# The first 12 units of an mLSTM cell with its MLP: hand-written order against a list schedule

## The chip, the cores and the metric

One core of a Trainium2 chip runs the whole program. The core has a tensor engine (TensorE, PE in the profile), a vector engine (VectorE, DVE), a scalar engine (ScalarE, ACT), a general engine (GpSimd, POOL) and a queue engine (SyncE, SP), each with its own queue of instructions that it works through in order. Transfers to and from memory (DMA) are handed out by SyncE, ScalarE or GpSimd. The metric is the device time of one execution in microseconds (us); less is better.

## The reference: an mLSTM cell, then an MLP with h - tanh(h)

Inputs are q, k, v and an output gate of shape (4, 8, 768, 40) (batches, heads, tokens, head size), gates i and f of shape (4, 8, 768), and the weights w_in (320 x 2048) and w_out (2048 x 320).

```python
for t in range(S):                       # per batch and head
    m_new = maximum(f[t] + m, i[t])
    f_stab, i_stab = exp(f[t] + m - m_new), exp(i[t] - m_new)
    C = f_stab * C + i_stab * outer(v[t], k[t])
    n = f_stab * n + i_stab * k[t]
    y[t] = sigmoid(o[t]) * (C @ q[t]) / maximum(abs(n @ q[t]), 1.0)
x = y as (3072 tokens, 320)
h = x @ w_in
out = (h - tanh(h)) @ w_out
```

All is float32 in the result. The weights arrive as 64-bit floating-point numbers, and the kernel turns their bits into float32 itself.

## The kernel before

**The cell in units.** The 768 tokens of a batch are cut into 6 chunks of 128; with 4 batches that makes 24 units (`NU`), unit n being chunk n // 4 of batch n % 4. Within a chunk the recurrence is written as matrix products. A unit goes through these steps:

- `load_unit` fetches its tiles: `kz`, `qz`, `v`, `k`, `o` and, from the second chunk on, `q2`.
- `scores`: 8 products of `kz` and `qz` into two banks (`ps`), then `mask` on VectorE writes the causal part to `P`.
- `prepare`: VectorE multiplies `v` with the gates' factors into `vs`, and lets the old state decay.
- `inter` (old state times q) and `intra` (`P` times `vs`): products into a bank `ph`.
- `open_gate` (sigmoid on ScalarE) and `gate` (VectorE: denominator, reciprocal, two products) give the unit's output `ys`.
- `update`: products of `vs` and `k` (`pc`), added to the state on VectorE.
- `turn`: three transposes of `ys` (`px`), copied by ScalarE to `xT`, the MLP's input for a group of two units.

The banks for `ph`, `pc`, `px` and the gates' products are the two of the pool `small` (`b0`, `b1`); every call takes the next one in turn.

**The gates.** `gate_rows` runs the scan for m on VectorE, and `gate_columns` turns the rows and makes the exponentials, both first for chunk 0 and then for chunks 1 to 5. VectorE, ScalarE and TensorE take turns in it.

**The weights.** The 2048 hidden features are cut into 16 blocks of 128, two of which are a pair p, 0 to 7. `convert` cuts each pair into five blocks (w_in in 256, 256 and 128 elements a partition, w_out twice in 320). Each block is fetched into `w64` and takes five VectorE steps (mask of the exponent, mask of the mantissa, `one`, `sign`, `product`) and two ScalarE steps (`w_r` and `w_e`). ScalarE's queue hands out the transfers of pair 0, GpSimd's those of the others.

**The MLP.** For a group g of two units (256 tokens) and a pair p, `up` makes h in the banks `ph_up`: four products over 128 features and two over 64. `shrink` makes h - tanh(h) as a polynomial: two squares on ScalarE (`z`, `q`) and two multiplies on VectorE (`gt`). `down` multiplies by w_out into `po`. For groups 0 to 3 the order of pairs is `RUNS`: it starts with group 0 and pair 0 and widens as units and weights become ready, so that a partial sum over some pairs is kept in `part` and added later. From group 4 to 10 all pairs of a group follow one another and `down_seven` replaces eight products by seven (`pS`); group 11 uses `down` again. Pairs are taken two at a time in 50 items; items 0, 1, 8 and 17 hold one. Items 0 to 17 are the 32 pairs of groups 0 to 3.

**What sets the order.** Each engine's order is the order in which the program writes its instructions; `Pinned` and `T` hold the framework to it. It is written in two ways. The start, units 0 to 2 with the gates and pair 0, is a list of calls by hand, with `awake(n)` in it: products of ones that nothing reads, of 512 columns, into the bank `ph0`. From then on a loop over items x writes `up` of item x and `down` of item x - 1 (`LAG` = 1), and `merge` lays other steps between them in proportion: those of the units (`cell_slot`, each spread over an interval of items), of the weights (spread over intervals before they are due) and of the gates. `Clock` delays single steps by a time counted in estimated matmul costs. From item 18 on, one bank of `small` is used for `pS`, and the units work with the other alone (`single`).

Of the kernel before, what the change touches and what calls it, by code (L numbers as in the profile page):

```python
# [59 lines left out]
L = 128  # L60
# [18 lines left out]
def kernel(  # L79
# [76 lines left out]

    B, NT, D, H, _ = qT.shape
# [85 lines left out]
    for n in range(2):  # L243
        load_unit(n, ("kz",))
        load_unit(n, ("qz",), A)
        load_unit(n, ("v",))
    load_gates(later)
    for name in "ko":
        for n in range(2):
            load_unit(n, (name,))  # L250


    ident = const.tile([128, 128], FP, name="ident")
# [31 lines left out]
    def awake(n):  # L285

        if not spare:
            spare.append(ps_h.tile([128, 512], FP, name="awake", tag="ph0"))
        row = diag.rearrange("p h t -> p (h t)")
        for _ in range(n):  # L290
            T.matmul(spare[0], row[:, 0:128], row[:, 0:512], start=True, stop=True)
# [13 lines left out]
    def gate_rows(c0, c1):  # L305

        t0, t1 = c0 * L, c1 * L
        at = slice(t0, t1)
        V.tensor_tensor_scan(out=m_sb[:, at], data0=f_sb[:, at], data1=i_sb[:, at],
                             initial=m_sb[:, t0 - 1:t0] if t0 else -1.0e30, op0=OP.add, op1=OP.max)  # L310
        if t0 == 0:

            V.memset(lf[:, 0:1], 0.0)
            t0 = 1
        V.tensor_tensor(out=lf[:, t0:t1], in0=f_sb[:, t0:t1], in1=m_sb[:, t0 - 1:t1 - 1], op=OP.add)
        V.tensor_tensor(out=lf[:, t0:t1], in0=lf[:, t0:t1], in1=m_sb[:, t0:t1], op=OP.subtract)
        V.tensor_tensor(out=i_sb[:, at], in0=i_sb[:, at], in1=m_sb[:, at], op=OP.subtract)


    def gate_columns(c0, c1, bank):  # L320
# [15 lines left out]

        def forget():
            V.tensor_copy(out=lfT[:, cs], in_=turned(0, lf))

        def admit():  # L340
            A.activation(out=ei[:, 2, cs], in_=turned(1, i_sb), func=AF.Exp)

        def since():
            V.tensor_single_scalar(inv[:, cs], sums_of(0, upto), 2 * DEEP, op=OP.max)
            V.tensor_reduce(out=least, in_=inv[:, cs].rearrange("p c n -> p (c n)"), axis=mybir.AxisListType.X, op=OP.min)
            A.activation(out=inv[:, cs], in_=inv[:, cs], func=AF.Exp, scale=-1.0)

        def until():
            A.activation(out=eS[:, cs], in_=sums_of(1, after), func=AF.Exp)
            V.tensor_tensor(out=ei[:, 0, cs], in0=ei[:, 2, cs], in1=inv[:, cs], op=OP.mult)  # L350
            V.tensor_tensor(out=ei[:, 1, cs], in0=ei[:, 2, cs], in1=eS[:, cs], op=OP.mult)

        def whole():
            half = sums_of(0, ones).rearrange("p c (b j two) -> p (c b) two j", two=2, j=HH)
            us = slice(c0 * B, c1 * B)
            A.activation(out=eT[:, us], in_=half[:, :, 1, :], func=AF.Exp)
            A.activation(out=eT[0:D, us], in_=half[0:D, :, 0, :], func=AF.Exp)
            V.tensor_single_scalar(least, least, TINY / DEEP, op=OP.mult)

        return forget, admit, since, until, whole  # L360


    w_in = const.tile([128, NK, DFF], FP, name="w_in")

    w_rest = const.tile([128, NP, 128], FP, name="w_rest")
    w_out = const.tile([128, NFF, DM], FP, name="w_out")

    def weights(dst, srcs, queue):
# [5 lines left out]
        def fetch():  # L374
            to = dst
            if src.dtype != FP:
                to = w["st"] = conv.tile([128, n], I64, name="w64", tag="w64", bufs=8)[0:p]
            for rows, cols, part in srcs:
                queue.dma_start(out=to[rows, cols], in_=part)

        def exponent():

            w["hi"] = w["st"].bitcast(I32).rearrange("p (n two) -> p n two", two=2)[:, :, 1]
            e = w["e"] = conv.tile([128, n], I32, name="w_e", tag="w_e", bufs=3)[0:p]
            V.tensor_single_scalar(e, w["hi"], 0x7FF00000, op=OP.bitwise_and)
            Clock.later(w["st"], 0.6, lambda: A.activation(out=e, in_=e, func=AF.Relu, scale=8.0, bias=rebias[0:p]))

        def mantissa():

            lo = w["st"].bitcast(U32).rearrange("p (n two) -> p n two", two=2)[:, :, 0]  # L390
            m, r = (conv.tile([128, n], I32, name=name, tag=name, bufs=3)[0:p] for name in ("w_m", "w_r"))
            w["m"], w["r"] = m.bitcast(FP), r.bitcast(FP)
            A.activation(out=w["r"], in_=lo, func=AF.Copy, scale=2.0 ** -52)
            V.tensor_scalar(out=m, in0=w["hi"], scalar1=0xFFFFF, scalar2=0x41000000, op0=OP.bitwise_and, op1=OP.bitwise_or)
# [5 lines left out]
        def sign():  # L400
            Clock.need(w["st"])
# [5 lines left out]
        if src.dtype == FP:  # L407
            return fetch, (), ()
        return fetch, (exponent, mantissa), (one, sign, product)

    WB = 2 * 128

    BLOCK = 5

    def convert():

        blocks = []
        for p in range(NP):
            queue = nc.gpsimd if p else A
            cols = slice(p * WB, (p + 1) * WB)  # L420
            fs = (2 * p, 2 * p + 1)
            every, slices = slice(0, 128), [slice(f * 128, (f + 1) * 128) for f in fs]
            blocks.append(weights(w_in[:, 0, cols], [(every, slice(0, WB), moe_w_in[0:128, cols])], queue))
            blocks.append(weights(w_in[:, 1, cols], [
                (every, slice(i * 128, (i + 1) * 128), moe_w_in[r:r + 128, slices[i]])
                for i, r in enumerate((FROM[2], FROM[1]))], queue))
            blocks.append(weights(w_rest[:, p, :], [
                (slice(i * HALF, (i + 1) * HALF), every, moe_w_in[r:r + HALF, slices[i]])
                for i, r in enumerate((FROM[1], FROM[2] + HALF))], queue))
            for f in fs:  # L430
                blocks.append(weights(w_out[:, f, :], [(every, slice(0, DM), moe_w_out[f * 128:(f + 1) * 128, :])], queue))
        steps = []
        for x in range(len(blocks) + 4):
            block = [blocks[i] if BLOCK <= i < len(blocks) else (lambda: None, (), ()) for i in (x, x - 2, x - 4)]
            steps.append([block[0][0], *block[2][2], *block[1][1]])
        return blocks[:BLOCK], steps

# [11 lines left out]
    def begin(n):  # L449
        t = un[n] = ld.pop(n)  # L450
        t["c"], t["b"] = divmod(n, B)
        t["hs"] = slice(t["b"] * H, (t["b"] + 1) * H)

        t["P"] = att.tile([L, 2, HH, L], FP, name="P", tag="P", bufs=4)
        t["qs"] = t.get("q2")
# [75 lines left out]
    def update(n, j):  # L531
        t = un[n]
        st = state[t["b"]][(t["c"] + 1) % 2]
# [3 lines left out]
        if j < HH - 1:  # L537
            return
# [7 lines left out]
    def turn(n, j):  # L546
# [4 lines left out]
        if j == NK:  # L551
            g, tt = divmod(n, GT)
            A.copy(out=xT[g % NX][:, :, tt * L:(tt + 1) * L], in_=t["px"])

    def cell_slot(s, o, x, single=False):


        steps = []
        if o is not None:
            prepare(o)  # L560
        if s is not None and s - 1 in un:
            prepare(s - 1)
# [4 lines left out]
        if x is not None and "turned" not in un[x]:  # L567
            turning = [(0.11, lambda j=j: turn(x, j)) for j in range(NK + 1)]
        else:
            turning = []  # L570
        if single:

            steps += turning
            if o is not None:
                for d in range(HH):
                    steps.append((0.22 if o >= B else 0.0, lambda d=d: inter(o, d)))
                    steps += [(0.22, lambda h=h: intra(o, h)) for h in (2 * d, 2 * d + 1)]
                steps.append((0.0, lambda: gate(o)))
                un[o]["turned"] = True
                pause = [(0.0, lambda: None)]  # L580
                steps += 5 * pause
                if o + B < NU:
                    steps += [(0.18, lambda j=j: update(o, j)) for j in range(HH)] + 4 * pause
                steps += [(0.11, lambda j=j: turn(o, j)) for j in range(NK + 1)] + 4 * pause
            return steps
        for d in range(HH):
            if o is not None:
                steps.append((0.22 if o >= B else 0.0, lambda d=d: inter(o, d)))
                steps += [(0.22, lambda h=h: intra(o, h)) for h in (2 * d, 2 * d + 1)]
                if d in (1, 2) and o + B < NU:  # L590
                    steps += [(0.18, lambda j=j: update(o, j)) for j in (2 * d - 2, 2 * d - 1)]
        if o is not None:
            steps.append((0.0, lambda: gate(o)))
        return steps + turning
# [10 lines left out]
    def sums_of_weights(p):  # L605
        t = wT[p] = conv.tile([128, 4, HM], FP, name="wT", tag="w64", bufs=8)
# [479 lines left out]
```

## Time and profile before

The median of three runs is 617.42 us (617.13 to 618.26). The profiled execution spans 614.3 us.

| engine | busy us | share | instructions |
|---|---|---|---|
| PE (matmul) | 564.4 | 92% | 3473 |
| PEld (weight load) | 472.7 | 77% | 3473 |
| DVE | 364.7 | 59% | 888 |
| ACT | 188.7 | 31% | 483 |
| POOL | 28.2 | 5% | 60 |

A float32 product shows as two matmul records, so "x24" for `ph_up` is 12 products. Most calls go through the helper at line 106 (VectorE and ScalarE) or line 129 (TensorE), so the profile is read by the names of tiles rather than by lines. In the profile's second part each digit is the busy share of one of 40 slices of 15.4 us, in tenths, and PEclk is the share of its full clock that TensorE was granted. In a table of stretches, "25.17 (x141)" is busy time and number of instructions. In a list of instructions the first number is the start, the second the time, and square brackets hold the idle time ahead of the instruction and what ended it.

### The profile page before, as it was taken

Reading aid. Unit: us, or ns where it says so; the run is one execution under the profiler, and the core shown is the slowest. Engines: PE = TensorE matmul, PEld = TensorE weight load, DVE = VectorE, ACT = ScalarE, POOL = GpSimd, SP = SyncE. Lnnn points to the kernel's source line nnn. Section 1 sums busy time; section 2 is a strip of 40 time slices with the busy share of each in tenths; the row PEclk is TensorE's granted clock in tenths of the full one; section 3 lists DMA queues with packets and bytes.
Section 4 is the critical chain, followed back from the end, with each engine's and each line's share of the span. In section 5 each row is a group of like instructions: output and inputs, shape, how many; then the busy total and the mean of one; then the engine's idle time right before and its main releaser. Section 6 shows DMA issues by size and latency. Waiting matters only on the chain.

```text
span 614.3 us, 9270 instructions
## 1 busy us (share of the span) xinstructions
PE 564.4 (92%) x3473; PEld 472.7 (77%) x3473; DVE 364.7 (59%) x888; ACT 188.7 (31%) x483; POOL 28.2 (5%) x60
## 2 busy tenths in 40 slices
PE   3948877899999899989999999999999999999996
PEld 1736766677777677767889899898988989888873
DVE  2686666666768855455876666556546456374421
ACT  1234333333435422321323232313132323133312
POOL 2021210001112000000000000000000000000000
PEclk7575589999999899999999999999999999999999
DMA  7653432323223301022211113011101000000000
GB/s 207 202 169 111 128 108 82 97 82 104 79 83 86 99 2 43 22 65 87 66 44 33 53 44 97 23 44 54 33 11 34 1 23 1 1 22 1 22 0 27
DMA packets 40868, 38.23 MB, mean 62 GB/s; under 512 B 3856, under 2 KB 38352, under 8 KB 40816
## 3 DMA queue, kind: packets, MB, share of 16 engines
q1 hardware_dynamic: 33000, 22.82, 12.8%
q0 software_dynamic: 2800, 9.18, 5.1%
q10 hardware_dynamic: 5016, 5.57, 2.7%
q8 instruction: 29, 0.48, 0.3%
q14 instruction: 23, 0.19, 0.1%
HBM read 33.62 MB, written 3.93 MB: 61 GB/s over the span
## 4 chain that ended last, share of the span: by engine, by line
PE 82%; DVE 12%; DMA 2%; issue 1%; ACT 1%; ACTq 0%; SPq 0%; DVEq 0%
PE ph_up L129 37%; PE pS L129 19%; PE po L129 11%; PE ph L129 8%; PE ps L129 4%; DVE gt L106 2%; PE pc L129 2%; DVE P L106 2%; PE px L133 2%; DMA kz<-in_kT 1%; PE awake L129 1%; DVE o L106 1%; DVE den L106 1%; DVE w_e L106 1%; DVE ys L106 1%
## 5 line engine op out<-in xcount | busy, mean ns | idle before, releaser
L129 PE MATMUL ph_up<-xT,w_in 128*128 128x256 f32 x768 | 206.8, 398 | 6.7 <-ACT xT L106 6.7
L129 PEld LDWEIGHTS ph_up<-xT,w_in 128*128 128x128 f32 x768 | 135.7, 194 | 20.4 <-ACT xT L106 7.2
L106 ACT ACTIVATE z<-ph_up 128x512 f32<-128x512 f32 (+1 forms) x100 | 57.1, 576 | 263.8 <-PE ph_up L129 180.0
L106 DVE SCALAR_TENSOR_TENSOR gt<-ph_up,z 128x512 f32<-128x512 f32 (+1 forms) x100 | 63.4, 663 | 99.4 <-ACT z L106 99.4
L129 PE MATMUL po<-w_out,gt 128*128 128x320 f32 x320 | 107.7, 459 | 1.4 <-DVE part L106 1.0
L129 PEld LDWEIGHTS ph<-vs,P 128*128 128x128 f32 x384 | 72.6, 212 | 20.0 <-issue 8.1
L106 DVE TENSOR_TENSOR P<-ps,upto 128x512 f32<-128x512 f32 x48 | 30.9, 686 | 75.8 <-PE ps L129 75.8
L129 PE MATMUL ph<-vs,P 128*128 128x41 f32 x384 | 65.5, 266 | 6.1 <-DVE vs L106 3.1
L129 PEld LDWEIGHTS po<-w_out,gt 128*128 128x128 f32 x320 | 55.4, 196 | 18.9 <-DVE part L106 3.5
L106 ACT ACTIVATE q<-z,tiny 128x512 f32<-128x512 f32 (+1 forms) x100 | 64.7, 701 | 0.0
L106 DVE SCALAR_TENSOR_TENSOR gt<-q,gt 128x512 f32<-128x512 f32 (+1 forms) x100 | 63.2, 661 | 0.0
L129 PE MATMUL pS<-wT,s 128*128 128x160 f32 x336 | 56.3, 304 | 0.0
L129 PE MATMUL ph_up<-xT,w_rest 64*128 64x256 f32 x384 | 55.5, 406 | 0.0
L129 PEld LDWEIGHTS pS<-wT,s 128*128 128x128 f32 x336 | 48.0, 190 | 0.0
L129 PEld LDWEIGHTS ph_up<-xT,w_rest 64*128 64x128 f32 x384 | 33.1, 187 | 14.2 <-issue 11.0
L106 ACT ACTIVATE w_e<-w_e,rebias 128x256 int32<-128x256 int32 (+2 forms) x40 | 20.3, 508 | 74.0 <-DVE w_e L106 73.9
L129 PE MATMUL pS<-w_out,gt 128*128 128x160 f32 x224 | 40.9, 314 | 0.0
L133 PE MATMUL px<-ident,ys 128*128 128x128 f32 x72 | 19.1, 291 | 19.5 <-DVE ys L106 18.7
L129 PEld LDWEIGHTS pS<-w_out,gt 128*128 128x128 f32 x224 | 32.0, 191 | 4.7 <-issue 4.3
L129 PEld LDWEIGHTS ph<-state,q 80*128 80x128 f32 x160 | 28.5, 195 | 6.5 <-issue 1.3
L129 PEld LDWEIGHTS ps<-qz,kz 40*128 40x128 f32 x384 | 28.9, 211 | 2.3 <-DVE P L106 0.8
L133 PEld LDWEIGHTS px<-ident,ys 128*128 128x128 f32 x72 | 10.2, 147 | 26.2 <-issue 22.2
(92 smaller groups left out, 562.9 us busy)
## 6 DMA issues: line engine op xcount, KB each, us to landing
w<-in_moe_w_out POOLq DMA_DIRECT2D x14, 320.0 KB, 3.3
kz<-in_kT SPq DMA_DIRECT2D x48, 80.0 KB
v<-in_v SPq DMA_DIRECT2D x24, 160.0 KB
k<-in_k SPq DMA_DIRECT2D x24, 160.0 KB
o<-in_o_gate SPq DMA_DIRECT2D x24, 160.0 KB
out<-ob ACTq DMA_DIRECT2D x24, 160.0 KB
qz<-in_qT SPq DMA_DIRECT2D x44, 80.0 KB
q<-in_qT SPq DMA_DIRECT2D x40, 80.0 KB
```

The source lines that it names most:

```text
L106: i = method(*args, **kwargs)
L129: return cls.keep(nc.tensor.matmul(*args, **kwargs))
L133: return cls.keep(nc.tensor.transpose(*args, **kwargs))
```

## The change

The part of the program up to item 17 gets its order from a list schedule. `Plan` holds operations, each with an engine (T, V, A, S for SyncE's loads, G for GpSimd's), an estimated duration, the operations it comes after, a rank, and buffers that it takes or gives back (`tokens`). `run` always takes the operation that can start first by the estimates, the lower rank among equals, and writes its instructions; so the written order of every engine follows from the plan. When TensorE has a gap in the plan, `idle` fills 60% of it with products of ones, which keep its clock up. The planned part covers units 0 to 11 (`PLANNED` = 12), the gates, all weights and items 0 to 17 but the last `down`; after it, the loop over items goes on from item 18 (`START`) with units 12 to 23, one unit to every two items.

Along with it:

- the weights of a pair are converted in two blocks of 640 elements a partition in place of five (`blocks_of`; w_in and the rest tile become one tile), all fetched through GpSimd's queue, with 4 buffers in place of 8;
- `v` of units 0 and 1 is fetched through GpSimd's queue, and `o` and `k` ahead of the later gates;
- `probe`, an exponential of one column at the start of ScalarE's queue, loads the activation table early;
- each step of `gate_rows`, `gate_columns`, `update`, `turn`, `shrink` and `down` can be called apart from the others, so that the plan can place it.

```diff
+    class Plan:
+        LAG = {"T": 0.25, "V": 0.07, "A": 0.12, "S": 1.7, "G": 1.9}
+        RATE = 0.23
...
+        def run(self, idle):
+            while self.todo:
+                t, _, _, op = min(((t, op["rank"], op["serial"], op) for op in self.todo if (t := self.start(op)) is not None),
+                                  key=lambda x: x[:3])
...
+                if op["engine"] == "T":
+                    idle(self.free["T"], t)
+                op["step"]()
+                op["end"] = self.free[op["engine"]] = t + op["us"]
...
-        load_unit(n, ("v",))
-    load_gates(later)
-    for name in "ko":
+        load_unit(n, ("v",), G)
+    for name in "ok":
         for n in range(2):
             load_unit(n, (name,))
+    load_gates(later)
...
+    probe = const.tile([128, 1], FP, name="probe")
+    V.memset(probe, 0.0)
+    A.activation(out=probe, in_=probe, func=AF.Exp)
...
-                to = w["st"] = conv.tile([128, n], I64, name="w64", tag="w64", bufs=8)[0:p]
+                to = w["st"] = conv.tile([128, n], I64, name="w64", tag="w64", bufs=4)[0:p]
...
+        return (weights(w_in[:, p, :], whole, nc.gpsimd),
+                weights(w_out[:, 2 * p:2 * p + 2, :].rearrange("p two n -> p (two n)"),
+                        [(every, slice(i * DM, (i + 1) * DM), moe_w_out[slices(2 * p + i, 1), :]) for i in range(2)], nc.gpsimd))
...
+    PLANNED = 12
+    START = item(FIRST * NP)
+    plan = Plan(small=("b0", "b1"), a=1, up=1, po0=1, po1=1, gt=2, z=1, P=4, vs=3, w64=4, w=2, ob=2)
...
+        u["scores"] = plan.add("T", 1.35, first_part, [u["qz"]], rank, [("a", held), ("P", held)])
+        u["mask"] = [plan.add("V", 0.68, lambda i=i: ready[1][i](), [u["scores"]], rank, give=[("a", held)] if i else ())
+                     for i in range(2)]
...
+        u["gate"] = plan.add("V", 1.5, lambda: gate(n), [op, u["open"], *of(n - 2, "turn")], rank, give=[("small", held)])
...
+            op = plan.add("G", 1.2 if k else 2.8, fetch, (), r, [("w64", held)], at=at, kb=655)
+            op = plan.add("V", 1.0, parts, [op], r, [("w", held)])
+            op = plan.add("A", 1.46, numbers, [op], r)
+            op = plan.add("V", 0.82, one, [op], r)
+            op = plan.add("V", 0.82, sign, [op], r, give=[("w64", held)])
+            converted[p, k] = plan.add("V", 0.82, product, [op], r, give=[("w", held)])
...
+    for x in range(START):
+        plan_item(x)
+    busy = []
+
+    def idle(t0, t1):
+        n = int((t1 - t0) * 0.6 / 0.215)
+        if n and not busy:
+            awake(n)
+        elif n and plan.tokens["a"] and plan.tokens["a"][0][0] <= t0:
+            stream(ps_a.tile([128, 512], FP, name="awake", tag="a0"), n)
+
+    plan.run(idle)
...
+    slots = [tuple(n if PLANNED <= n < NU else None for n in (s, s - 1)) for s in range(PLANNED, NU + 1)]
+    last = item((NG - 1) * NP) - 2.0
+    for i, slot in enumerate(slots):
+        x0, x1 = (START + (last - START) * j / len(slots) for j in (i, i + 1))
+        begins[int(x0)].append((slot, x0, x1))
```

The calls by hand at the start, `convert`, the spreading of weights over items and the two-bank form of `cell_slot` are removed.

## The prediction

> **What bounds the kernel now.** I read the span by slices first, then busy time by stage, then the order of TensorE's instructions inside a stage, and last the waits of the start. The slices show two regimes:
>
> ```profile
> PE   3948877899999899989999999999999999999996
> DVE  2686666666768855455876666556546456374421
> PEclk7575589999999899999999999999999999999999
> ```
>
> From slice 19 on TensorE (PE) is at 9 and its clock is full. In the first five slices (77 us) it is often idle and its clock is at 0.5 to 0.8. Busy time by stage, with the cut at 288.08 us, where item 18 (the first after the 32 pairs of groups 0 to 3) begins its first product:
>
> ```profile
> core 0: us, PE busy (x) PEld busy (x) DVE busy (x) ACT busy (x) POOL busy (x), PEclk, DMA share, GB/s
> 0.00:40.00 40.00, 25.17 (x141) 17.94 (x141) 20.86 (x62) 7.88 (x20) 6.05 (x19) 0.74 0.68 202
> 40.00:100.00 60.00, 47.07 (x260) 39.87 (x260) 39.34 (x116) 24.71 (x65) 9.69 (x18) 0.66 0.36 105
> 100.00:200.00 100.00, 91.43 (x546) 72.12 (x547) 70.07 (x182) 38.32 (x101) 11.87 (x22) 1.00 0.32 94
> 200.00:288.00 88.00, 80.55 (x428) 60.84 (x427) 51.55 (x126) 25.79 (x66) 0.54 (x1) 0.96 0.15 46
> 288.00:581.00 293.00, 293.00 (x1986) 262.44 (x1985) 174.96 (x391) 83.67 (x212) 0.00 (x0) 1.00 0.11 34
> ```
>
> Busy 91 of 100 us looks full. It is not, because a busy matmul can be one that waits in the pipe or runs on half the clock. So I price TensorE's work by the distance from start to start where it runs without a pause. The end of the chain gives the large products: 24 records (two pairs of blocks) take 4.52 us, so 2.26 us a pair up, and 16 records take 4.50 us, so 2.25 us a pair down:
>
> ```profile
> 585.76 4.52 PE ph_up L129 x24
> 590.27 4.50 PE po L129 x16
> ```
>
> TensorE's own order at full clock gives the small ones: 0.14 us for a `ph` of P and vs, 0.18 for a `pc`, 0.19 for a `ph` of the state, 0.99 for all scores of a unit.
>
> ```profile
> 91.95 0.31 PE L129 MATMUL ph<-vs,P 128*128 128x41 f32 x2
> 92.09 0.35 PE L129 MATMUL pc<-vs,k 128*80 128x82 f32 x2
> 92.27 0.64 PE L129 MATMUL ph_up<-xT,w_in 128*128 128x256 f32 x2
> ...
> 93.36 0.35 PE L129 MATMUL ph<-state,q 80*128 80x82 f32 x2
> 93.55 0.64 PE L129 MATMUL ph_up<-xT,w_in 128*128 128x256 f32 x2
> ...
> 95.23 1.06 PE L129 MATMUL ps<-qz,kz 40*128 40x128 f32 x16
> 96.22 0.41 PE L129 MATMUL ph<-vs,P 128*128 128x41 f32 x2
> ```
>
> A unit of the first chunk therefore costs 0.99 + 8 x 0.14 + 4 x 0.18 + 0.33 (three transposes) = 3.2 us, a later one 4 x 0.19 = 0.76 more, 3.9 us. By 288 us the kernel has done 32 pairs up (72.3), 31 down (69.8), 13 units (4 x 3.2 + 9 x 3.9 = 47.9), parts of units 13 and 14 (two sets of scores, one set of `ph`: 3.9) and the gates' products (some 2): **196 us of work in 288**. So 92 us are lost in the first stage. The same count after 288 gives 64 pairs up 144.6, 1 + 8 pairs down 20.3, 56 pairs of seven products (28 records in 4.00 us, so 2.00 a pair) 112, and 9 to 10 units' worth 36: 313 us in 326. That stage is at its bound.
>
> What makes the loss at the start: ScalarE.
>
> ```profile
> 4.71 6.89 ACTq L106 DMA_DIRECT2D w<-in_moe_w_in  x5
> 11.63 1.08 ACTq L106 DMA_DIRECT2D w<-in_moe_w_out  x2
> 12.74 1.28 ACT L106 ACT_TABLE_LOAD   x1 [12.74 <-DMA w<-in_moe_w_in]
> 14.04 0.20 ACT L106 ACTIVATE ei<-gate 128x32 f32<-128x32 f32 x1
> ```
>
> ```profile
> 14.38 0.60 PE L129 MATMUL gate<-lfT,after 128*128 128x32 f32 x2 [7.68 <-ACT inv L106]
> ```
>
> ScalarE spends 8 us handing out weight transfers, then loads its table; the gates' exponentials wait for it, TensorE 7.68 us, and the first mask is at 18.14. Later TensorE has gaps of 2 to 6 us in front of `px`, `ph` and `ph_up`, each ended by VectorE (`ys`, `vs`) or by `xT`; the first product up starts at 40.72. Between 40 and 70 us the clock is half, so work there costs double.
>
> **What the Trainium skill says.** "Perfetto Trace Analysis", section Identifying the Most-Contended Engine: busy time of matmuls is a bad measure of how near the engine is to its limit. The trace agrees (100 to 288 us: 91% busy, yet 85% by start-to-start cost: 28 pairs up 63, 29 down 66, units 31, so 160 of 188). "TensorE: Matmul & The Clock Gate", Part 1: after an idle window of some 3.4 us the clock falls to half, and a busy window restores it. The trace agrees: 0.50 from 10 to 20 and from 50 to 70 us, 1.00 from 100 on. "VectorE: DVE Perf Modes", the section on the TRN2 errata: each instruction pays a fixed cost, so fewer and larger ones are cheaper. The trace agrees: 128, 256 and 320 elements of one conversion step take 282, 416 and 481 ns, about 150 ns plus 1.03 ns an element. "ScalarE: Activation LUTs", What ACT_TABLE_LOAD costs: about 1283 ns; the trace has 1283.
>
> **The change, part by part.**
> - Start. Weights go out from GpSimd, and `probe` loads the table before the gates need it. Removed: the 7.68 us wait. The mask still needs `kz`, which landed at 11.06 us, and VectorE starts in earnest at about 10 to 12 instead of 18. Worth about 7 us. GpSimd issues at 0.54 us each, 7 a pair, beside nothing that waits for it; the first weights may land some us later than the plan supposes, since `v` and 1.8 MB of other loads share 200 GB/s.
> - Conversion: 16 blocks of 640 elements for 40 of 128 to 320. Extrapolated from those rows: 2 x 0.47 + 3 x 0.81 = 3.4 us of VectorE a block, 54 for all, against 73 now: 19 less (busy time, of which some overlaps: count 17). ScalarE 16 x 1.6 = 26 against 37. ScalarE's share lies beside other work.
> - Order. The written order up to item 17 is replaced by a list schedule that gives each engine the operation that can start first. It adds no instructions except ones for gaps. Work in the stage: TensorE 72.3 + 69.8 + 12 units (4 x 3.2 + 8 x 3.9 = 44.0) + 2 = 188 us. VectorE now: 181.8 us busy to 288 by stage; less 17 for conversion and about 8 for the units that move later: 157.
> - Ones in gaps: 60% of each gap the plan expects. They cost nothing where the gap is real, and keep the clock. Where the plan is wrong they delay: `awake` x31 was 13.8 us busy, mostly at half clock. From 0 to 10 us; I take 3, inside the slip below.
> - Units 12 and 13 move behind item 18: 3.9 for a whole unit and 3.9 for the parts done early are added after the cut: 326.2 + 7.8 = **334 us**. A slot shrinks from 2.47 items to 2.0. With one bank for the units, each step waits for VectorE; the pauses between keep that, so I add nothing (bound 0 to 6).
>
> How soon can the planned stage end? At first VectorE decides, because a pair of blocks for a group needs both a converted pair and two finished units. When three groups and three pairs are ready, VectorE has done gates 5, six units 26, three conversions 20 and nine pair-items at 1.9 (four multiplies 1.4, an eviction 0.5) 17: 68 us of rows, or about 60 without overlap. At 88% use from 10 us on this is at 10 + 68 = 78 us. TensorE has then had 9 x 4.51 + 6 units 21 = 62 us to do. What is left, 188 - 62 = 126 us, exceeds what VectorE has left (157 - 60 = 97), so TensorE decides; at 88%, a little over the 85% that the stage from 100 us on shows now, 143 us. Sum 221, and I add 9 for late weights, ones and steps whose order suits only the plan: **230 us against 288**. Then 230 + 334 = 564 of span, and 3 us from span to device time (617.4 - 614.3): **567 us**.
>
> **The rivals.**
> - The plan holds almost as written. VectorE at 95% until 73 us, then TensorE at 97%: 130, so 203 + 334 + 3 = 540. For it: VectorE is only 63% busy now up to 100 us, so the room is there. Against: engines take their queues in order, and one late transfer holds all behind it. Chance 0.15.
> - A new wait takes the old one's place: VectorE's queue, now full, holds up masks, evictions and `gate`, and `small` has two banks for `ph`, `pc` and `px`. VectorE at 70%: 96 us; TensorE at 80%: 157; 253 + 334 + 3 = 590. For it: even now VectorE ends most of TensorE's gaps. Chance 0.22.
> - Slower than before. The order fits the chip so badly that VectorE is used no more than now, 55%: 119 us, and then TensorE at 75% with ones in the wrong places: 168; 287 + 334 + 3 = 624. For it: TensorE's whole order is fixed by estimated durations, and the move of two units alone costs 8 us. Against: 92 us of slack have to be kept for it. Chance 0.11.
>
> **How the numbers follow.** Forecast 567 with chance 0.52. The range 545 to 604 holds the forecast, the second rival and the better part of the space between; outside are most of the first rival and the slower case. Faster 0.88 (all but the last), within 0.2% 0.01, slower 0.11.
>
> **What would show it.** First mask near 11 us in place of 18.14, first `ph_up` between 24 and 32 in place of 40.72. TensorE's clock near 1.0 from some 20 us on, with `awake` records between. Conversion rows of 640 elements near 0.81 and 0.47 us. First `pS` near 245 in place of 304.6, and from there to the end about as long as now plus 8. VectorE 85 to 90% busy between 15 and 80 us. Wrong would be: TensorE waits of more than 3 us for weights (conversions behind the transfers), `awake` records right ahead of work that was ready, or new waits after item 18 on the one small bank.

## The result and the profile after

The changed kernel takes 573.17 us (median of four, 569.43 to 576.87) against 617.36 us (617.13 to 618.26): a ratio of 0.928, with a 95% interval of 0.922 to 0.935. The forecast was 567 us within 545 to 604, so it held; the result lies 6 us above it. Some executions are slow for a reason outside the kernel; medians are of all runs, ratios leave the slow ones out.

The slices of the profile after show where the time came from: TensorE's idle slices at the start are gone, and from the third slice on the engine is at 8 or 9. Products of ones are part of that in both kernels (31 records each, 13.8 us busy before and 12.1 after).

```profile
PE   8788899999999999999999999999999999999995
DVE  4789778788875425678656665665664555544421
PEclk9789799899999999999999999999999999999999
```

Item 18 begins at 233.35 us (288.08 before). TensorE's order there, before and after, shows down products of an earlier item, and then the first products of item 18:

```profile
286.92 1.32 PE L129 MATMUL po<-w_out,gt 128*128 128x320 f32 x4
288.08 2.32 PE L129 MATMUL ph_up<-xT,w_in 128*128 128x256 f32 x10
...
228.94 4.57 PE L129 MATMUL po<-w_out,gt 128*128 128x320 f32 x16
233.35 4.68 PE L129 MATMUL ph_up<-xT,w_in 128*128 128x256 f32 x24
```

Busy time by stage, first from item 18 on in the kernel before, then all of the changed one, cut there and at the 80 us of the forecast's first part. The last three numbers of a row are the granted clock, the share of DMA and GB/s:

```profile
core 0: us, PE busy (x) PEld busy (x) DVE busy (x) ACT busy (x) POOL busy (x), PEclk, DMA share, GB/s
288.08:614.30 326.22, 320.15 (x2100) 281.89 (x2098) 182.82 (x406) 91.98 (x232) 0.00 (x0) 1.00 0.11 32
...
0.00:80.00 80.00, 69.16 (x422) 51.36 (x425) 60.05 (x138) 34.83 (x77) 22.71 (x48) 0.89 0.65 184
80.00:233.35 153.35, 152.73 (x847) 119.53 (x847) 102.84 (x206) 51.75 (x122) 11.87 (x21) 0.98 0.24 73
233.35:570.10 336.75, 329.28 (x2207) 291.75 (x2205) 190.66 (x426) 92.60 (x237) 0.00 (x0) 1.00 0.12 36
```

So the planned stage is 54.7 us shorter than its counterpart and the rest is 336.8 us, 10.5 longer than the 326.2 of before, since it now holds more of units 12 and 13: 44 us in all. VectorE was busy 60.2 us in the first 100 us before; now it is busy as long in 80 us. From 80 us on TensorE hardly pauses.

At the start, the list of instructions of all engines has the table load at 4.66 us (12.74 before), the first mask at 10.31 (18.14 before), and the first product up at 28.59 (40.72 before). After, and then before:

```profile
4.66 1.28 ACT L106 ACT_TABLE_LOAD   x1 [4.66 <-issue]
10.31 1.29 DVE L106 TENSOR_TENSOR P<-ps,upto 128x512 f32<-128x512 f32 x2 [0.38 <-PE ps L129]
28.59 2.60 PE L129 MATMUL ph_up<-xT,w_in 128*128 128x256 f32 x12
...
18.14 1.29 DVE L106 TENSOR_TENSOR P<-ps,upto 128x512 f32<-128x512 f32 x2 [2.63 <-PE ps L129]
40.72 1.22 PE L129 MATMUL ph_up<-xT,w_in 128*128 128x256 f32 x2 [5.58 <-ACT xT L106]
```

The groups by shape show the two-block conversion, total and mean of one:

```profile
L106 DVE SCALAR_TENSOR_TENSOR w_e<-w,w_e 128x640 int32<-128x640 int32 x16 | 12.9, 815 | 0.0
L106 DVE SCALAR_TENSOR_TENSOR w_r<-w_m,w_r 128x640 f32<-128x640 f32 x16 | 12.8, 814 | 0.0
L106 DVE TENSOR_SCALAR w_m<-w 128x640 int32<-128x640 int32 x16 | 7.7, 483 | 0.0
```

### The profile page after: what moved, and what is told of

It reads as the page before. It is cut to its first block, busy times and chain, and to the rows that moved or that the text cites. A ratio compares the mean times of both kernels' runs of the same rounds, so it can differ in the third digit from the quotient of the medians.

```text
span 570.1 us, 9133 instructions
## 1 busy us (share of the span) xinstructions
PE 551.2 (97%) x3473; PEld 462.6 (81%) x3476; DVE 353.5 (62%) x769; ACT 179.2 (31%) x436; POOL 34.6 (6%) x69
## 4 chain that ended last, share of the span: by engine, by line
PE 92%; DMA 3%; ACT 1%; DVE 1%; ACTq 1%; issue 0%; SPq 0%; DVEq 0%
PE ph_up L129 39%; PE pS L129 20%; PE po L129 16%; PE ph L129 9%; PE ps L129 4%; DMA qz<-in_qT 3%; PE pc L129 2%; PE px L133 2%; ACTq L106 1%; ACT q L106 0%; ACT z L106 0%; SPq L288 0%; DVE gt L106 0%; PE gate L129 0%; ACT L106 0%
## 5 line engine op out<-in xcount | busy, mean ns | idle before, releaser
L129 PE MATMUL ph_up<-xT,w_in 128*128 128x256 f32 (+1 forms) x1152 | 248.7, 394 | 2.0 <-ACT xT L106 1.1
L129 PEld LDWEIGHTS ph_up<-xT,w_in 128*128 128x128 f32 (+1 forms) x1152 | 170.4, 190 | 34.9 <-issue 12.2
L129 PE MATMUL po<-w_out,gt 128*128 128x320 f32 x320 | 99.3, 455 | 2.5 <-DVE gt L106 2.0
L129 PEld LDWEIGHTS ph<-vs,P 128*128 128x128 f32 x384 | 58.2, 194 | 4.2 <-ACT o L106 0.5
L129 PE MATMUL ph<-vs,P 128*128 128x41 f32 x384 | 57.2, 264 | 0.0
L129 PE MATMUL ph<-state,q 80*128 80x82 f32 x160 | 31.4, 278 | 0.0
L129 PE MATMUL ps<-qz,kz 40*128 40x128 f32 x384 | 27.2, 277 | 2.4 <-DMA qz<-in_qT 2.4
L459 POOL DMA_DIRECT2D w<-in_moe_w_in x40 | 22.8, 576 | 73.5 <-DVE w_e L106 25.2
L106 ACT COPY xT<-px 128x384 f32<-128x384 f32 x24 | 11.4, 476 | 47.6 <-PE px L133 47.6
L129 PEld LDWEIGHTS pc<-vs,k 128*80 128x80 f32 x160 | 19.9, 172 | 3.4 <-issue 0.5
```

Source lines behind the costliest of these rows:

```text
L106: i = method(*args, **kwargs)
L129: return cls.keep(nc.tensor.matmul(*args, **kwargs))
```

## The experiments

Each ratio is to the kernel before, run on the same chip. The changed kernel's own repeated run, 0.9215, was on the chip of the next three experiments. Those further down ran on other chips, so their ratios are set beside 0.9215 only by way of the kernel before. Its runs also scatter: 569.4 to 576.9 us in the result, 569.4 to 573.2 here. Differences of a few us are read with that in mind.

**The changed kernel again.**

> The changed kernel as it is, on the same chip as the three that follow, as their measure. Both theories: 0.928 of before, 569 to 577 us; item 18 begins near 233 us, the clock is low in some five short stretches.

Measured: 570.98 us, ratio 0.9215 (0.9172 to 0.9257). First `pS` at 246.09 us. This is the measure for the next three.

**No ones in the gaps.**

```diff
-        n = int((t1 - t0) * 0.6 / 0.215)
+        n = 0
```

> The changed kernel without products of ones in the gaps. Theory (the ones hold the clock up while the first units leave gaps, up to 28 us): the scores and products up to about 35 us run at half clock, item 18 begins 4 to 8 us later, total 577 to 581. Rival (the ones do nothing, since VectorE and transfers decide at the start): within 2 us of the changed kernel. Other rival (ones delay work that was ready): 2 to 4 us faster.

Measured: 571.04 us, ratio 0.9221 (0.9176 to 0.9266). The first rival holds: the ones are worth nothing in time. They keep the clock up only in part. Without them the first three sets of scores take 2.15, 2.30 and 2.08 us; with them 1.16, 1.54 and 1.35 us in the run of the result, but 1.16, 1.55 and 2.08 us in the repeated one. That run had half the clock from 15 to 30 us, although TensorE was busy throughout and 12 products of ones were among its work:

```profile
core 0: us, PE busy (x) PEld busy (x) DVE busy (x) ACT busy (x) POOL busy (x), PEclk, DMA share, GB/s
15.00:30.00 15.00, 15.00 (x72) 11.45 (x73) 8.71 (x23) 5.05 (x10) 3.04 (x6) 0.50 0.84 224
...
24.57 2.08 PE L129 MATMUL ps<-qz,kz 40*128 40x128 f32 x16
```

The first product up begins at 29.16 us without ones, and at 28.59 and 31.17 in the two runs with them: TensorE's speed there is not what it waits for.

**Five blocks a pair, in the plan.** `blocks_of` returns the five blocks of before, with 8 buffers `w64` and 3 of each temporary, and the plan gets their durations and issue counts.

```diff
-            op = plan.add("V", 0.82, one, [op], r)
...
+            step = 0.15 + 0.00105 * n
...
+            op = plan.add("V", step, one, [op], r)
```

> The changed kernel with each pair converted in five blocks again, planned with durations to match; same order by plan, same queue. Theory (VectorE decides until about 80 us, TensorE after that): of the 17 to 19 us of VectorE that come back only what falls into the first 80 us counts, four or five pairs of eight, at most 9 us: total 576 to 582. Rival 1 (VectorE decides in the whole planned stage): 588 to 592. Rival 2 (conversion is hidden anyway, the order is all): within 2 us of the changed kernel.

Measured: 575.58 us, ratio 0.9287 (0.9238 to 0.9336). That is 4.6 us over the changed kernel by the medians, just below the theory's 576 to 582. The intervals overlap a little: by them the loss is between nothing and some 8 us. The profiled run, at 570.47 us the fastest of six, lost nothing (item 18 at 231.94 us, 232.70 in the repeated run above). So the first rival (588 to 592) is refuted, the second (within 2 us) is not quite ruled out, and of some 19 us of VectorE work less than half reaches the end.

**The later gates early.**

```diff
-    later_tokens, later_states = gates(1, NT, 1.5, 12.0, in_po)
+    later_tokens, later_states = gates(1, NT, -0.7, 12.0, in_po)
```

> The changed kernel with the gates of chunks 1 to 5 ranked ahead of units 2 and later (rank -0.7 for 1.5), so that the stretch from 52 to 63 us, where TensorE does little but gates and falls to half clock, moves to the first 30 us. Theory (that stretch costs 5 to 8 us, and the start has room for it): total 565 to 570. Rival (VectorE's work is only moved, units 2 and 3 and the first products come later): 573 to 580.

Measured: 570.10 us, ratio 0.9193 (0.9144 to 0.9242): no difference that can be told, just outside the theory's range and short of the rival's. Its first pair up is done at 35.1 us, later than in the two runs of the changed kernel (31.2 and 33.8), and its eighth at 91.3 (91.5 and 94.1): what the gates no longer cost later they cost at the start. The rival's mechanism, without its loss.

**The start's cure alone, in the kernel before.**

```diff
+    probe = const.tile([128, 1], FP, name="probe")
+    V.memset(probe, 0.0)
+    A.activation(out=probe, in_=probe, func=AF.Exp)
...
-            queue = nc.gpsimd if p else A
+            queue = nc.gpsimd
```

> The kernel before with the start's cure alone: pair 0's weights go out from GpSimd and one early exponential loads the table; order and conversion as before. Theory (the 7.68 us wait of the gates is on the path, since all that follows in the fixed order waits for it): 7 us less, 609 to 612. Rival (later waits for VectorE and transfers take its place): within 2 us of 617.

Measured: 613.32 us, ratio 0.9894 (0.9867 to 0.9921): 6.5 us less by the ratio (5 to 8 by its interval). The size fits the theory; the trace does not show its mechanism in full. It is of a run of 614.95 us, one of the slower ones, and has the first mask 7.6 us earlier, but the first product up only 2.4 us and item 18 only 1.5 us earlier:

```profile
10.54 1.29 DVE L106 TENSOR_TENSOR P<-ps,upto 128x512 f32<-128x512 f32 x2 [1.89 <-PE ps L129]
38.35 1.22 PE L129 MATMUL ph_up<-xT,w_in 128*128 128x256 f32 x2 [5.58 <-ACT xT L106]
286.58 2.32 PE L129 MATMUL ph_up<-xT,w_in 128*128 128x256 f32 x10
```

The 5.58 us wait for `xT` ahead of the first product up is as long as before. So in this run later waits took most of what the start won, which is the rival; where the faster runs won their time stays open.

**Ones in the gaps of the kernel before.** Fourteen ahead of the first product up, six at items 1 and 2, seven ahead of the transposes of units 2 to 7.

```diff
+            if 2 <= n < 8 and "qs" in t and tc_gaps:
+                ones_in_gap(7)
```

> The kernel before with products of ones in its gaps: 14 ahead of the first product up, 6 at items 1 and 2, and 7 ahead of the transposes of units 2 to 7. Order and conversion as before. Theory (the low clock of some 68 us is mostly an effect of the bad order, and VectorE decides there): 2 to 8 us less, 609 to 615. Rival 1 (the clock is the main loss of the early stage): 20 to 30 us less, 587 to 597. Rival 2 (ones only get in the way): 617 to 622.

Measured: 617.38 us, ratio 0.9988 (0.9973 to 1.0003). No difference can be told. The theory and the first rival are missed; the number lies at the lower edge of the second rival's range. The trace shows both why nothing is won and what the ones cost. The second pair up begins 3.6 us later than before (75.42 us against 71.80) and then takes 3.8 us in place of 6.3:

```profile
71.80 1.14 PE L129 MATMUL ph_up<-xT,w_in 128*128 128x256 f32 x2
77.43 0.70 PE L129 MATMUL ph_up<-xT,w_rest 64*128 64x256 f32 x4
...
75.42 0.64 PE L129 MATMUL ph_up<-xT,w_in 128*128 128x256 f32 x2
78.50 0.70 PE L129 MATMUL ph_up<-xT,w_rest 64*128 64x256 f32 x4
```

It ends at 79.2 us against 78.1, the eighth pair at 126.8 against 126.9, the twelfth at 160.2 against 157.7. The kernel is never ahead, so the 9 us at the start of which the expectation for the transposes below speaks are not in the traces. Faster matmuls are given back as waits.

**A plan with wrong durations.**

```diff
             self.serial += 1
+            us = us * (0.6, 1.4, 1.0, 0.7, 1.3)[self.serial * 7 % 5]
```

> The changed kernel with a plan that believes wrong durations: each is taken times 0.6, 1.4, 1.0, 0.7 or 1.3 in turn. The operations are the same, only their order and the ones change. Theory (after 80 us TensorE has more work ready than it can do, so the order needs no exact times): 573 to 583. Rival (the gain lies in the calibrated durations): 590 to 615.

Measured: 573.77 us, ratio 0.9296 (0.9260 to 0.9332), 3 us over the changed kernel by the medians, 5 by the ratios. The theory holds: an order from durations up to 40% off keeps nearly all of the gain.

**Small products between large ones.** Products of the second part and of `update` become single operations from unit 5 on, and the plan prefers a large product behind a small one where one is ready.

```diff
-                t, _, _, op = min(((t, op["rank"], op["serial"], op) for op in self.todo ...
+                t, _, _, op = min(((t, op["rank"] + 1000.0 * (op["small"] and self.small), op["serial"], op) for op in self.todo ...
```

> The changed kernel with the products of a unit's second part and of its state update (from unit 5 on) laid one by one between large products, where the plan has one ready. Theory (in the changed kernel 12 such products in a row take 2.7 us and 4 of pc 0.7, while between large ones they cost 0.14 to 0.19 us each, 1.9 and 0.6; seven planned units): 4 to 7 us less than the changed kernel, 564 to 567. Rival (the unit's chain gets longer by the large products in between, and VectorE and the groups wait for it): 571 to 580.

Measured: 571.29 us, ratio 0.9209 (0.9172 to 0.9245): nothing gained, and nothing lost, so the rival's range holds without its reason. Laid side by side, TensorE's order explains it. The changed kernel, in a row:

```profile
133.69 1.16 PE L129 MATMUL ps<-qz,kz 40*128 40x128 f32 x16
134.78 0.45 PE L129 MATMUL ph<-state,q 80*128 80x82 f32 x2
135.06 0.58 PE L129 MATMUL ph<-vs,P 128*128 128x41 f32 x4
...
137.48 0.78 PE L129 MATMUL pc<-vs,k 128*80 128x82 f32 x8
138.19 1.14 PE L129 MATMUL ph_up<-xT,w_in 64*128 64x256 f32 x8
```

The experiment, laid between:

```profile
129.25 0.68 PE L129 MATMUL ph_up<-xT,w_in 128*128 128x256 f32 x2
129.77 0.31 PE L129 MATMUL ph<-vs,P 128*128 128x41 f32 x2
129.91 0.68 PE L129 MATMUL ph_up<-xT,w_in 128*128 128x256 f32 x2
```

In a row, 12 products take 137.48 - 134.78 = 2.70 us. A `ph` of P and vs costs 0.20 us in a row (two in the 0.41 us to the next start, 135.47). Between large ones it seems to take 0.14 us, but its large neighbour then takes 0.52 us (129.25 to 129.77) instead of the 0.43 of a dense run (two records, 0.216 us apart, from 585.81 us of the kernel before). So the small one costs 0.20 to 0.23 us in both orders; the distance from start to start had booked a part of it on its neighbour.

**Units held back; weights held back.** Two orders from the plan with the readiness of the old one. (Here an item's first product also comes after that of the item before, which alone leaves the order as it was.)

```diff
-        u["scores"] = plan.add(..., [("a", held), ("P", held)])
+        pace = (0, 0, 32, 54, 64, 78, 95, 110, 127, 137, 160, 183)
+        u["scores"] = plan.add(..., [("a", held), ("P", held)], at=pace[n])
```

> The changed kernel with the scores of each unit held in the plan until the time at which they began in the kernel before (32, 54, 64, 78, 95, 110, 127, 137, 160, 183 us for units 2 to 11). Only the order changes, nothing waits for a clock on the chip. Theory (the pace of the units in the written order is what held the old first stage back): two thirds of the order's gain of some 33 us are lost, 585 to 600. Rival (any order that the plan finds is good as long as ready work comes first): 571 to 578.

Measured: 585.42 us, ratio 0.9441 (0.9397 to 0.9485): 14 us lost, first `pS` at 260.86, so all of it in the planned stage. The time is at the lower edge of the theory's range, but the loss is less than half of some 33 us, not the two thirds that the theory named.

```diff
-            op = plan.add("V", 1.0, parts, [op], r, [("w", held)])
+            pace = (0, 54, 80, 117, 154, 184, 201, 233)
+            op = plan.add("V", 1.0, parts, [op], r, [("w", held)], at=pace[p] - 5.0 + 1.5 * k)
```

> The changed kernel with each pair's conversion held in the plan until about the time at which it was done in the kernel before (54, 80, 117, 154, 184, 201, 233 us for pairs 1 to 7); only the order changes. Theory (units and pairs both set how much there is to do for TensorE; pairs weigh more since the last is needed by all groups): 590 to 605. Rival (conversion was early enough before): 571 to 578.

Measured: 597.65 us, ratio 0.9638 (0.9596 to 0.9680): 26 us lost, first `pS` at 272.33. The theory holds, and pairs weigh more than units. With few pairs converted, the plan runs units back to back and has no large products to lay with them; TensorE is busy the whole time from 46 to 67 us, at half clock (0.51). Its order there has products at nearly twice the usual time, 2.08 us for scores that take 1.06 to 1.16 elsewhere:

```profile
60.14 0.70 PE L129 MATMUL ph<-state,q 80*128 80x82 f32 x2
60.63 0.99 PE L129 MATMUL ph<-vs,P 128*128 128x41 f32 x4
61.55 2.08 PE L129 MATMUL ps<-qz,kz 40*128 40x128 f32 x16
```

**Transposes first, in the kernel before.**

```diff
+        steps += turning
         for d in range(HH):
...
-        return steps + turning
+        return steps
```

> The kernel before with one edit: in the two-bank part a slot's three transposes come at its start and not right behind the gate of the next unit, whose bank they take over in turn. Theory (TensorE's nine waits for ys, 18.7 us in all, come from that bank and hand themselves on: while TensorE waits VectorE has nothing, then VectorE works while TensorE waits): 8 to 16 us less, 602 to 610. Rival (the waits only move to the next step, as with the ones, whose 9 us at the start were gone by 160 us): within 3 us of before.

Measured: 617.43 us, ratio 0.9983 (0.9954 to 1.0012): the rival. My theory of the bank falls. The list of who waited for whom from 30 to 288 us, with total, times and longest, has the wait undiminished, before and then with the edit:

```profile
PE px L133 <- DVE ys L106: 18.7, 9, 3.0
PE px L133 <- DVE ys L106: 20.2, 9, 4.1
```

TensorE waits there for `ys` itself: VectorE's queue is behind, not the bank.

**Three cures by hand, in the kernel before.** The start, the transposes and

```diff
+    due = [0.7 * x for x in due]
```

> The kernel before with three edits by hand: the start's cure, the transposes at the start of a slot, and the weights' steps due at 0.7 of their items. Theory (the three add up as far as VectorE has room): 595 to 605. Rival 1 (order by hand at fixed places can't use the room; only the start's 6 us count): 610 to 613. Rival 2 (they reach what the plan reaches): below 585.

Measured: 613.07 us, ratio 0.9877 (0.9832 to 0.9922), no more than the start's cure alone. That fits the first rival: VectorE is busier between 100 and 200 us (76.6 us against 70.1), and TensorE less (86.3 against 91.4).

## Why the prediction was right, and where it was off

**What bounds the kernel.** Right. 54.7 us came out of the first stage and none out of the second; 10.5 of them came back there, with the work that moved.

**Start.** The numbers were right: 6.5 us alone, 7 forecast; first mask 10.31 (near 11 forecast), first product up 28.59 (24 to 32). The path was only half right. "Removed: the 7.68 us wait" took it that what the start wins reaches the end. In the trace of the start's cure 7.6 us at the first mask had become 1.5 at item 18, so the agreement of 6.5 with 7 may be partly luck. And "ScalarE spends 8 us handing out weight transfers" was a misreading of merged rows. One by one, the seven took 0.33 to 0.60 us each, 3.5 us in all; for the rest of the 8 us ScalarE's queue stood still between them:

```profile
5.25 0.59 ACTq L106 DMA_DIRECT2D w<-in_moe_w_in  x1
8.80 0.33 ACTq L106 DMA_DIRECT2D w<-in_moe_w_in  x1
10.28 0.56 ACTq L106 DMA_DIRECT2D w<-in_moe_w_in  x1
```

The chain of the first 22 us puts the transfer at 11.08 behind the landing of `kz` at 11.06 (4.21 + 6.85):

```profile
4.21 6.85 DMA kz<-in_kT
11.06 0.02 issue
11.08 0.51 ACTq L106
```

**Conversion.** The size was right: 0.815 and 0.483 us an instruction (0.81 and 0.47 forecast), 54.1 us in all on VectorE. Its share of the end is about 4.6 us, and 0 to 8 by the intervals. That suits a part that counts only while VectorE decides, but it is too uncertain to show it.

**Order.** The mechanism was right and is the largest part. Of 44 us some 6.5 belong to the start, some 4.6 to the blocks, none to the ones; about 33 remain for the order (27 to 39 by the intervals of the two). That is a remainder: the parts need not add up, and it also holds the moved loads of `v`, `o` and `k` and the fewer buffers, which were not tried alone. What supports it: holding back units or conversions in the plan loses 14 and 26 us, the kernel before gains nothing from the transposes first or, beyond the start's cure, from these with earlier weights, and wrong durations in the plan cost little. So the gain is not one wait removed. In the old order TensorE waited for VectorE (`px` for `ys`, 18.7 us from 30 us on) and VectorE for TensorE (`P` for `ps`, 18.7 us from 15 to 100 us) by turns; in the new one that last wait, shown here as it was before, is not in the list for those 85 us.

```profile
DVE P L106 <- PE ps L129: 18.7, 6, 6.9
```

**How soon the planned stage ends.** 233.4 us, 230 forecast, but by two errors that cancel. VectorE's share was right: 60 us of work by 78 us forecast, 60.05 by 80 measured. What TensorE had done by then was not. The step "TensorE has then had 9 x 4.51 + 6 units 21 = 62 us to do" was oversized: by 80 us it had done 6 pairs up and 5 down (13.6 + 11.3) and 7 sets of scores with the second parts of some five units, about 45 us at the same prices. By then VectorE had three pairs converted and a fourth begun, six units masked and five gated: about what the forecast wanted, but with six pair-items in place of nine. Why its 60 us bought less is not worked out. The rest then went better than the 88% assumed: 143 us of work in 153, 93%, slip included. That the two errors cancel is luck.

**Price of a unit.** "A unit of the first chunk therefore costs 3.2 us, a later one 3.9" was too low. In a row it is 1.09 + 2.70 + 0.71 + 0.33 = 4.8 us for a later unit, and laying its small products between large ones did not make it cheaper. With 0.9 us more a unit (some 0.5 in the first chunk), the stage from 80 us on is some 97% full rather than 93%. The first stage of before then held some 206 us of work, not 196, so its slack was some 80 us, not 92; and the second was nearer its bound than 313 of 326 suggested.

**Second stage.** 334 us forecast, 336.8 measured. The 7.8 us for moved units lacked 0.9 us for each of some two units; the rest of the 2.8 is within what I left open for the shorter slots. TensorE has one wait of 0.8 us there, so the feared waits on the one small bank did not come.

**Ones.** They cost nothing that can be told (3 us forecast, inside the slip), and I gave their effect on the clock no number of its own; it is nil in time. The remark that work at half clock "costs double" was true of TensorE and, as far as the two experiments with ones show, beside the point for the end. That a busy window restores the clock did not always hold: it stayed at half through 15 and 21 us of busy TensorE, as shown above.

**VectorE 85 to 90% busy between 15 and 80 us** was wrong: 52.96 of 65 us, 81%. **Clock near 1.0 from 20 us on** was half right: there are still stretches at half clock, and the mean from 20 to 80 us is 0.89, 0.82 in the repeated run. **First `pS` near 245**: 246.74.

The sum is 233.4 + 336.8 + 1.8 (from the span to device time in that execution) = 571.9 us, rounded. The 3 us that the forecast added for the last part mixed the span of one execution with the median of others: the profiled one took 616.0 us, 1.7 over its span.

Two readings of the lines were a little off, without weight for the forecast: VectorE was busy 60.2 of the first 100 us before, not 63%, and the clock "1.00 from 100 on" is 0.96 from 200 to 288 us.

What stays open: which feature of the old order did most harm. Moving the transposes, alone and with the due times, did not find it.

## What to carry to other kernels

When the busiest engine looks 91% busy, price its work by dense runs of the same instructions before believing it; here that found some 80 us of slack in one stage and next to none in the next. Where several in-order queues wait for one another by turns, mending one wait can move it: of 7.6 us won at the first mask 1.5 were left at item 18. Here the gain came when the order was made as a whole, ready work first on every engine, for which rough durations sufficed. And price a small instruction from runs in a row or from the neighbour's delay as well; between large ones the distance from start to start flatters it.

## What the runs showed of the hardware that I had not expected

- A busy TensorE does not always get its clock back. With weights held back it was busy 21.0 of 21 us from 46 to 67 us with small products, at a granted clock of 0.51; in the repeated run of the changed kernel 15.0 of 15 us from 15 to 30 us, with 12 products of ones among them, at 0.50.
- The clock column reads 1.00 for 8 to 32 us of the kernel without ones, yet its scores take 2.08 to 2.30 us there, twice the 1.06 to 1.16 us at full clock. The record of the clock seems to begin later than the run; durations of a known instruction are the safer guide.
- A queue that hands out transfers can stand still between them: of the 8.0 us for seven weight transfers on ScalarE only 3.5 went into handing out, 0.33 to 0.60 us each, about as long as on GpSimd (0.54 to 0.58 on average). What stands behind them in the queue waits too, as the table load did until 12.74 us.
